# Loading q and k in whole 4 KB runs, in transfers of 512 KB, in a sliding-window attention and mixture-of-adapters kernel

## The chip, the core and the metric

The kernel runs on one core of one Trainium2 chip. The metric is the device time of one execution in microseconds (us). A core has five engines that work side by side: TensorE (PE in the profile, with its weight loads as PEld), VectorE (DVE), ScalarE (ACT), GpSimd (POOL) and SyncE (SP). Sixteen DMA engines move data between the chip's memory and the core.

## The reference

Sliding-window attention over 8 batches, 8 heads, 576 rows and 64 columns, followed by a mixture of eight rank-16 adapters of which each row takes the best two:

```python
scores = scale * np.matmul(q, k.transpose(0, 1, 3, 2))
mask = np.abs(pos[:, None] - pos[None, :]) <= 32
scores = np.where(mask, scores, -1000000000.0)
attn = softmax(scores)                       # rows
x = (attn @ v) with heads beside each other  # 4608 x 512
logits = x @ w_gate                          # 8 experts
topk, w = best two experts of a row, softmax of their logits
out = x + sum over the two of w * ((x @ A[e]) @ B[e])
```

The inputs q, k and v are float32, 9.4 MB each; the output is 9.4 MB.

## The kernel before, in words

**Tiling.** The 8 batches are taken as 4 stages `s`; each stage holds the batches `s` and `s + 4` (the two groups `g`) side by side. Along the rows a batch is cut into 256-row pieces `t` (two for each stage, `t` = 0 to 7) and a remainder piece `t` = 8 (`XT`) that gathers the last rows (for q the first and the last rows) of all heads and batches. For each piece there is a q tile and a k tile; both come as *halves* `hf` = 0 and 1.

**Loading q and k** (`load_qk`, `run_parts`). A partition belongs to a run of 16 rows of one head, 4 KB of memory in one piece. A half takes 8 of these 16 rows, so each partition's packet has 2 KB, and a half is two transfers (one for each group) of 256 KB, four of 128 KB for q of the remainder. They are issued on SP's queue (L317) into one of nine buffers `raw`. Each half is then cast to float16 into `c16` (L328 on ACT, L330 on DVE or POOL), turned by eight transposing matmuls (L338), and copied from PSUM into `qT` or `kT` (L355). `ends` (L365) copies the remainder's q rows to where the stage's first and last blocks need them.

**Loading v** (`load_v`). Four transfers for each piece, issued on POOL's queue (L383), read 8 KB of float32 for each of 32 partitions and write 4 KB of float16 into `v16`; a VectorE transpose (L391) makes `vt` of it. There are 36 such transfers.

**Computing.** `score` puts mask (L426) and scores (L432) into two PSUM banks, and ACT takes the exponential into `PT` (L438). `pv` multiplies `PT` with `vt` (L478), and DVE normalises into `xa` or `xb` (L490, L497). `moe` transposes these rows (L523, L182), computes gate and first adapter product (L563), the gate on DVE and ACT (L573 to L604), transposes again (L613), computes the second product and adds x (L637, L640), and evicts into one of four buffers `ob` (L648, L651); SP stores them (L658), two transfers for each `ob`.

**Order.** Nothing is scheduled at run time. Every step is an `Op`; `Plan.give` issues them in the order of the table `ORDER`, with the engine from `ON` and the buffer from `HOME`. These three tables were found by a search. Every engine works through its own steps in that order and waits where a step isn't ready, so what stands behind a waiting instruction on the same engine waits too. Transfers on SP's queue rotate over eight completion semaphores, shared with the three weight loads on ACT's queue: a transfer is issued only after the eighth transfer before it has landed.

Of the kernel before, what the change touches and what calls it, by code (L numbers as in the profile page):

```python
# [16 lines left out]
D = 64  # L17
# [86 lines left out]
def kernel(  # L104
# [14 lines left out]
    POOLS = {"B": 8, "raw": 9, "c16": 6, "v16": 3, "xq": 1,  # L119
# [5 lines left out]
    def many(name, shape, dt, pool=sb):  # L125
# [3 lines left out]
        "raw": many("raw", [128, 2, 8 * D], F32),  # L129
# [158 lines left out]
    def run_parts(w, t, f):  # L288

        r = []  # L290
        for g in range(2):
            x = grows[w][g]
            if t < XT:
                r0 = 256 * (t % 2) + (32 if w == "q" else 0)
                i = x[t // 2, :, r0:r0 + 256].rearrange("h (n f r) d -> f n h (r d)", f=2, r=8)[f]
                r.append((g, 0, 128, i))
            elif w == "k":
                i = x.rearrange("b h n d -> (b h) n d")[:, 512:576].rearrange(
                    "u (n f r) d -> f u n (r d)", f=2, r=8)[f]
                r.append((g, 0, 128, i))  # L300
            else:
                for e in range(2):
                    i = x.rearrange("b h n d -> (b h) n d")[:, 544 * e:544 * e + 32].rearrange(
                        "u (n f r) d -> f u n (r d)", f=2, r=8)[f]
                    r.append((g, 64 * e, 64, i))
        return r

    def load_qk(w, t):
# [4 lines left out]
        dst = kT[t] if w == "k" else xq if t == XT else qT[t // 2]  # L313
        for hf in range(2):
            raw = buf("raw", f"raw{w}{t}_{hf}")
            for n, (g, p0, np_, src) in enumerate(run_parts(w, t, hf)):
                op("SP", 0.46, lambda g=g, p0=p0, np_=np_, src=src, raw=raw: nc.sync.dma_start(  # L317
                    out=ap(raw)[p0:p0 + np_, g], in_=src),
                   bufs=[raw], make=[(w, t, "raw", hf)],
                   prio=(-80 + due + late if t else -200 + late) + 0.1 * hf + 0.01 * n,  # L320
                   dma=DMA_MB / 4 * np_ / 128, desc=np_)
            c16 = buf("c16", f"{w}16_{t}_{hf}")

            def cast(eng, raw=raw, c16=c16):
                o = ap(c16).rearrange("p r (g d) -> p r g d", g=2)
                i = ap(raw).rearrange("p g (r d) -> p r g d", d=D)
                if eng == "ACT":
                    nc.scalar.copy(out=o, in_=i)  # L328
                else:
                    (nc.vector if eng == "DVE" else nc.gpsimd).tensor_copy(out=o, in_=i)  # L330
            op({"DVE": 0.68, "ACT": 1.03} if t == 0 else CAST, 0,
               cast, bufs=[raw, c16],
               need=[(w, t, "raw", hf)], make=[(w, t, hf, "16")], prio=due - 30 + late + 0.1 * hf)
# [345 lines left out]
def BY_PE(s, w, j):  # L679
# [36 lines left out]
)  # L716
ON = (
    "001110000000100000000100010001000000010000000010000001000100000000000000000101000100000100"
    "001000010000000110010000000000000000100000000000000000001000100010000000000000000010000000"
    "000000000100000000000001000000000000000000000000010001000000000000000101000000000000000000"  # L720
    "001000001000000000000010000000000000000000000100000000000000000000010000100000100000010010"
    "000100100000001000000000011000001000000000000010000100000000000100000100000100010010000000"
    "000000000000000000010000000000000000000000100000000000000000000000000000000000000100000000"
    "0000000000000000000000000000000000000000100000000001000"
)
HOME = (
# [13 lines left out]
)  # L740


# [1 line left out]
_INS = ['q', 'k', 'v', 'moe_w_gate', 'moe_A', 'moe_B']  # L744
_OUTS = [((4608, 512), 'float32')]


# [23 lines left out]
```

## Time and profile before

| | |
|---|---|
| median of 3 runs | 150.35 us (149.16 to 151.33) |
| the profiled execution: its time, its span | 149.54 us, 147.8 us |
| PE busy | 117.6 us (80%) |
| DVE, ACT, POOL busy | 90.4, 84.9, 51.6 us |
| moved by DMA | 33.91 MB in 19,783 packets |
| read from memory, written to it | 28.85 MB, 9.44 MB |

The profile is of one execution. Busy time is the time in which an engine runs an instruction; the span is that of the instructions on the core, and the execution's own time is 1.7 us longer. A DMA packet is what one DMA engine moves in one go; the DMA share is the packets' time over the time of all 16 engines, and as packets overlap a little it can pass 1. The chain of work is followed back from the last instruction: at each step to what released it.

### The profile page before, as it was taken

How to read it: one execution, taken by the hardware profiler on the slowest of the kernel's cores; microseconds unless marked ns; L12 is line 12 of the kernel's file. 1: busy time of each engine (PE TensorE's matmuls, PEld its weight loads, DVE VectorE, ACT ScalarE, POOL GpSimd, SP SyncE). 2: the span in 40 equal slices, each digit the busy share in tenths (PEclk: the TensorE clock that was granted, in tenths of full speed). 3: DMA queues.
4: the chain of work that ended last, by engine and by line, in shares of the span. 5: the costliest groups of instructions: out<-in, count | busy, mean ns of one | idle time of the engine just before them, and what ended most of it. 6: DMA issues, size and time to landing. Idle time of an engine off the chain costs nothing.

```text
span 147.8 us, 5212 instructions
## 1 busy us (share of the span) xinstructions
PE 117.6 (80%) x2206; PEld 85.0 (58%) x2206; DVE 90.4 (61%) x185; ACT 84.9 (57%) x123; POOL 51.6 (35%) x88
## 2 busy tenths in 40 slices
PE   4932279869399789599899999999998999976730
PEld 2302265656198657486488794677685674954300
DVE  4010067080568567997997764786958589958530
ACT  4102434937644896568666839659697588542530
POOL 7960002853388225623529139940200000000000
PEclk9995556999968999959999999999999999999995
DMA  4999999999999999999999999999911030940484
GB/s 128 256 225 254 266 254 297 283 258 254 271 273 273 275 240 277 268 286 347 326 278 322 302 301 290 145 266 293 332 40 49 27 113 0 320 150 0 170 311 160
DMA packets 19783, 33.91 MB, mean 230 GB/s; under 512 B 4656, under 2 KB 4656, under 8 KB 19760
## 3 DMA queue, kind: packets, MB, share of 16 engines
q1 hardware_dynamic: 15680, 28.32, 63.5%
q0 software_dynamic: 2752, 4.72, 18.0%
q10 hardware_dynamic: 1328, 0.54, 1.6%
q8 instruction: 17, 0.28, 0.8%
q14 instruction: 6, 0.05, 0.1%
HBM read 28.85 MB, written 9.44 MB: 259 GB/s over the span
## 4 chain that ended last, share of the span: by engine, by line
PE 54%; DMA 20%; DVE 13%; ACT 3%; issue 3%; POOL 2%; SPq 0%; DVEq 0%; ACTq 0%; POOLq 0%
PE banks L432 11%; DMA raw<-in_q_dram 9%; PE banks L338 8%; PE banks L478 8%; PE banks L426 6%; DMA v<-in_v_dram 6%; PE banks L523 6%; PE banks L637 5%; PE banks L563 5%; DMA raw<-in_k_dram 4%; DVE xb L497 4%; PE banks L640 3%; DVE vt L391 3%; PE banks L613 2%; DVE ob L648 1%
## 5 line engine op out<-in xcount | busy, mean ns | idle before, releaser
L330 POOL CAST c<-raw 128x1024 f16<-128x1024 f32 x26 | 26.7, 1045 | 50.5 <-DMA raw<-in_k_dram 27.4
L438 ACT ACTIVATE PT<-banks 128x1024 f16<-128x1024 f32 x36 | 35.7, 1026 | 7.9 <-PE banks L432 7.4
L338 PEld LDWEIGHTS <-c 128*128 128x128 f16 x288 | 20.2, 111 | 12.6 <-ACT c L328 8.5
L338 PE MATMUL banks<-swap,c 128*128 128x128 f16 x256 | 21.2, 242 | 6.9 <-ACT c L328 4.7
L391 DVE STREAM_TRANSPOSE vt<-v 128x1024 f32<-128x1024 f32 x9 | 18.4, 2061 | 7.2 <-DMA v<-in_v_dram 7.2
L432 PE MATMUL banks<-qT,kT 64*64 64x128 f16 (+1 forms) x576 | 22.2, 218 | 0.6 <-ACT qT L355 0.4
L432 PEld LDWEIGHTS <-kT 64*64 64x64 f16 x576 | 16.8, 108 | 10.2 <-issue 9.3
L478 PE MATMUL banks<-vt,PT 64*128 64x65 f16 x832 | 17.8, 192 | 6.0 <-DVE vt L391 3.0
L478 PEld LDWEIGHTS <-PT 64*128 64x128 f16 x832 | 14.9, 95 | 9.4 <-issue 7.3
L383 POOL DMA_DIRECT2D v<-in_v_dram x36 | 19.6, 559 | 0.7 <-DVE sm L574 0.6
L497 DVE TENSOR_TENSOR xb<-banks,rc 128x768 f16<-128x768 f32 x16 | 15.3, 958 | 3.4 <-PE banks L523 3.0
L637 PE MATMUL banks<-Bw,zT 128*128 128x512 f16 x40 | 14.4, 381 | 1.7 <-ACT zT L182 1.7
L426 PE MATMUL banks<-mask,twice 64*128 64x512 f16 x72 | 14.9, 390 | 0.5 <-ACT qT L355 0.4
L328 ACT CAST c<-raw 128x1024 f16<-128x1024 f32 x7 | 7.3, 1044 | 12.2 <-DMA raw<-in_k_dram 6.7
L355 ACT COPY qT<-banks 128x512 f32<-128x512 f32 x14 | 8.1, 588 | 10.5 <-PE banks L338 8.1
L648 ACT COPY ob<-banks 128x1024 f32<-128x1024 f32 x11 | 11.1, 1020 | 4.0 <-PE banks L640 3.4
L182 ACT COPY xT<-banks 128x512 f32<-128x512 f32 x15 | 8.6, 588 | 5.9 <-PE banks L523 5.2
L330 DVE CAST c<-raw 128x1024 f16<-128x1024 f32 x3 | 2.1, 694 | 15.9 <-DMA raw<-in_q_dram 14.9
L355 ACT COPY kT<-banks 128x512 f32<-128x512 f32 x13 | 7.7, 589 | 6.5 <-PE banks L338 6.5
L563 PE MATMUL banks<-WA,xT 128*128 128x136 f16 x160 | 10.8, 223 | 0.0
L497 DVE TENSOR_TENSOR xa<-banks,rc 128x640 f16<-128x640 f32 (+1 forms) x12 | 10.3, 862 | 0.3
L563 PEld LDWEIGHTS <-xT 128*128 128x128 f16 x160 | 9.6, 98 | 0.6
(61 smaller groups left out, 130.5 us busy)
## 6 DMA issues: line engine op xcount, KB each, us to landing
raw<-in_k_dram SPq DMA_DIRECT2D x36, 256.0 KB, 7.1
raw<-in_q_dram SPq DMA_DIRECT2D x32, 256.0 KB, 7.4
out_dram<-ob SPq DMA_DIRECT2D x24, 256.0 KB, 4.3
v<-in_v_dram POOLq DMA_DIRECT2D x36, 128.0 KB, 7.2
out_dram<-ob SPq DMA_DIRECT2D x16, 192.0 KB, 3.2
raw<-in_q_dram SPq DMA_DIRECT2D x8, 128.0 KB, 7.1
ob<-in_moe_A_dram ACTq DMA_DIRECT2D x1, 256.0 KB, 3.7
ob<-in_moe_B_dram ACTq DMA_DIRECT2D x1, 256.0 KB, 5.4
```

The lines of the kernel that those rows point to most:

```text
L330: (nc.vector if eng == "DVE" else nc.gpsimd).tensor_copy(out=o, in_=i)
L338: nc.tensor.matmul(out=ap16(tp)[:, 128 * r:128 * r + 128], lhsT=ap(c16)[:, r], rhs=swap if t < XT else ident, is_transpose=True, start=Tru ...
L355: (nc.vector.tensor_copy if eng == "DVE" else nc.scalar.copy)(out=o, in_=i)
L383: op("POOL", 0.5, lambda p0=p0, src=src: nc.gpsimd.dma_start(out=ap(v16)[p0:p0 + 32], in_=src), bufs=[v16], make=[("v", t, "16")], prio=-6 ...
L391: nc.vector.transpose(out=o, in_=i)
L426: nc.tensor.matmul(out=p[:, 4 * j:4 * j + 4], lhsT=twice[m], rhs=bcast(mask[m], 1, 4), start=True, stop=False)
L432: nc.tensor.matmul(out=p[m, h, c0:c0 + hi - lo], lhsT=ap(kT[t])[m, 64 * sl:64 * sl + 64], rhs=ap(qT[s])[m, h, lo:hi], start=False, stop=h ...
L438: op("ACT", act(1024), lambda: nc.scalar.activation(out=ap(pt)[:, :, 64:192].rearrange("m i (x b r) -> m i x b r", b=2, r=16), in_=ap(ps). ...
L478: nc.tensor.matmul(out=ap(po)[:, 512 * g + VD * j:512 * g + VD * j + VD], lhsT=ap(PT[ti])[m, pos, off:off + 128], rhs=ap(vt[t])[m, sl, 0:V ...
L497: nc.vector.tensor_tensor(out=o, in0=i, in1=ap(rc)[:, 0:n].to_broadcast([128, n, 2, D]), op=ALU.mult)
L563: nc.tensor.matmul(out=ap(pz)[:, o:o + ER + E], lhsT=ap(xT)[:, i, c, :], rhs=WA[:, c, :], start=(c == 0), stop=(c == 3))
L637: nc.tensor.matmul(out=o, lhsT=ap(zT)[:, j + i], rhs=Bw, start=True, stop=not by_pe)
```

## The change

A q or k piece is loaded whole. `run_parts` no longer takes the half `f`: each partition's packet is the whole run of 16 rows, 4 KB, and a transfer has 512 KB (256 KB for q of the remainder). A `raw` buffer is twice as large (8 KB for each partition) and there are five of them, where there were nine. The two casts of a piece read the two halves of one `raw` buffer, and both need all transfers of the piece. Casts, transposes, evictions and everything behind them keep their shapes and their number. 76 load transfers of q and k become 40. The three tables `ORDER`, `ON` and `HOME` come from a new search, so the order of all steps, the engine of some, and the buffers are others. Line numbers behind `run_parts` are three lower.

```diff
-    POOLS = {"B": 8, "raw": 9, "c16": 6, "v16": 3, "xq": 1,
+    POOLS = {"B": 8, "raw": 5, "c16": 6, "v16": 3, "xq": 1,
...
-        "raw": many("raw", [128, 2, 8 * D], F32),
+        "raw": many("raw", [128, 2, 16 * D], F32),
...
-    def run_parts(w, t, f):
+    def run_parts(w, t):
...
-                i = x[t // 2, :, r0:r0 + 256].rearrange("h (n f r) d -> f n h (r d)", f=2, r=8)[f]
+                i = x[t // 2, :, r0:r0 + 256].rearrange("h (n r) d -> n h (r d)", r=16)
                 r.append((g, 0, 128, i))
...
+        raw = buf("raw", f"raw{w}{t}")
+        for n, (g, p0, np_, src) in enumerate(run_parts(w, t)):
+            op("SP", 0.46, lambda g=g, p0=p0, np_=np_, src=src: nc.sync.dma_start(
+                out=ap(raw)[p0:p0 + np_, g], in_=src),
+               bufs=[raw], make=[(w, t, "raw")],
+               prio=(-80 + due + late if t else -200 + late) + 0.01 * n,
+               dma=DMA_MB / 2 * np_ / 128, desc=np_)
         for hf in range(2):
-            raw = buf("raw", f"raw{w}{t}_{hf}")
-            for n, (g, p0, np_, src) in enumerate(run_parts(w, t, hf)):
-                op("SP", 0.46, lambda g=g, p0=p0, np_=np_, src=src, raw=raw: nc.sync.dma_start(
-                    out=ap(raw)[p0:p0 + np_, g], in_=src),
-                   bufs=[raw], make=[(w, t, "raw", hf)],
...
-            def cast(eng, raw=raw, c16=c16):
+            def cast(eng, hf=hf, c16=c16):
                 o = ap(c16).rearrange("p r (g d) -> p r g d", g=2)
-                i = ap(raw).rearrange("p g (r d) -> p r g d", d=D)
+                i = ap(raw).rearrange("p g (f r d) -> p f r g d", f=2, d=D)[:, hf]
...
-               need=[(w, t, "raw", hf)], make=[(w, t, hf, "16")], prio=due - 30 + late + 0.1 * hf)
+               need=[(w, t, "raw")], make=[(w, t, hf, "16")], prio=due - 30 + late + 0.1 * hf)
...
 ORDER = (
...
 ON = (
...
 HOME = (
```

More of the change, by code (lines that the diff above doesn't have):

```diff
@@ L294, in run_parts @@
                 r0 = 256 * (t % 2) + (32 if w == "q" else 0)
-                i = x[t // 2, :, r0:r0 + 256].rearrange("h (n f r) d -> f n h (r d)", f=2, r=8)[f]
+                i = x[t // 2, :, r0:r0 + 256].rearrange("h (n r) d -> n h (r d)", r=16)
                 r.append((g, 0, 128, i))
[L297 to L305, printed above, removed]
+                continue
+            u = x.rearrange("b h n d -> (b h) n d")
+            rows = [(0, 512, 576)] if w == "k" else [(0, 0, 32), (64, 544, 576)]
+            for p0, a, b in rows:
+                i = u[:, a:b].rearrange("u (n r) d -> u n (r d)", r=16)
+                r.append((g, p0, 2 * (b - a), i))
         return r
@@ L313, in load_qk @@
         dst = kT[t] if w == "k" else xq if t == XT else qT[t // 2]
-        for hf in range(2):
-            raw = buf("raw", f"raw{w}{t}_{hf}")
-            for n, (g, p0, np_, src) in enumerate(run_parts(w, t, hf)):
-                op("SP", 0.46, lambda g=g, p0=p0, np_=np_, src=src, raw=raw: nc.sync.dma_start(
-                    out=ap(raw)[p0:p0 + np_, g], in_=src),
-                   bufs=[raw], make=[(w, t, "raw", hf)],
-                   prio=(-80 + due + late if t else -200 + late) + 0.1 * hf + 0.01 * n,
-                   dma=DMA_MB / 4 * np_ / 128, desc=np_)
+        raw = buf("raw", f"raw{w}{t}")
[5 more added lines that the diff above has]
+               dma=DMA_MB / 2 * np_ / 128, desc=np_)
+        for hf in range(2):
             c16 = buf("c16", f"{w}16_{t}_{hf}")
-            def cast(eng, raw=raw, c16=c16):
+            def cast(eng, hf=hf, c16=c16):
                 o = ap(c16).rearrange("p r (g d) -> p r g d", g=2)
-                i = ap(raw).rearrange("p g (r d) -> p r g d", d=D)
+                i = ap(raw).rearrange("p g (f r d) -> p f r g d", f=2, d=D)[:, hf]
                 if eng == "ACT":
@@ L684 @@
 ORDER = (
[31 rows of a table removed]
[29 rows of a table added]
 )
 ON = (
[L718 to L724, printed above, removed]
+    "000001101001100000000000010000000010000101000100100011000100000000000000000011101100001010"
+    "000000100000000100000010100000000000000000010010000000000001001001000000100000000000000000"
+    "000000000010000000000000000000000000100100100000000000000000000000000100000000000000000010"
+    "100000000100000000000001000000000000011000000000100000001000000000000000001010000000000000"
+    "010000000100000000000000000011100001000000100000000010000100000000000000000000100000000010"
+    "010000000000000000000000000010000000000000010000000000000000000000000000000000000000000001"
+    "00000000000001000"
 )
 HOME = (
[13 rows of a table removed]
[12 rows of a table added]
 )
```

85 rows, old and new, of tables (HOME, ORDER) are left out of this document.

## The prediction

> **What bounds the kernel now.** I read the page first, for engines and DMA queues.
>
> ```profile
> span 147.8 us, 5212 instructions
> PE 117.6 (80%) x2206; PEld 85.0 (58%) x2206; DVE 90.4 (61%) x185; ACT 84.9 (57%) x123; POOL 51.6 (35%) x88
> ...
> DMA  4999999999999999999999999999911030940484
> ...
> q1 hardware_dynamic: 15680, 28.32, 63.5%
> q0 software_dynamic: 2752, 4.72, 18.0%
> ...
> q8 instruction: 17, 0.28, 0.8%
> ```
>
> The DMA engines are full from the second of 40 slices to the 29th, about 107 us; only then have the last loads landed. PE is busy 80% of the whole. So I ask where PE is short of work, with the windows cut at the end of the warm-up matmuls, the first score, the start of PE's dense part, and the last evictions (columns: length, busy time of PE, PEld, DVE, ACT, POOL, granted clock, DMA share, GB/s):
>
> ```profile
> 8.60:23.70 15.10, 6.00 (x51) 4.72 (x50) 4.49 (x9) 4.51 (x6) 1.45 (x3) 0.58 1.07 259
> 23.70:64.00 40.30, 32.42 (x693) 25.73 (x693) 24.98 (x43) 25.77 (x38) 21.99 (x32) 0.92 1.07 266
> 64.00:128.00 64.00, 62.12 (x1333) 45.29 (x1332) 49.34 (x101) 46.19 (x65) 20.71 (x27) 0.99 0.76 224
> 128.00:147.80 19.80, 10.67 (x140) 6.74 (x132) 9.74 (x27) 6.02 (x11) 0.00 (x0) 0.91 0.49 166
> ```
>
> Three regimes. Up to 23.7 us the loads bound: DMA share 1.07, PE idle 9.1 us. From 23.7 to 64 loads and PE share the bound: PE idles 7.9 us while the DMA share stays at 1.07. From 64 to 128 PE is the bound, with 1.9 us idle in 64. The last 19.8 us are a chain of small steps with no load in it. The chain of waits, in order of time, shows the first two:
>
> ```profile
> 1.47 6.26 DMA raw<-in_k_dram
> 7.75 6.95 DMA raw<-in_q_dram
> 14.72 6.84 DMA raw<-in_q_dram
> 21.62 1.05 ACT c L328
> 22.72 1.03 PE banks L338 x8
> 23.76 0.54 PE banks L426
> ...
> 29.67 8.80 DMA v<-in_v_dram
> 38.50 2.05 DVE vt L391
> 40.59 0.70 PE banks L478 x34
> ```
>
> Faster loads can therefore win time only ahead of about 64 us: what PE idles there is the most that they can give.
>
> **What a packet costs.** From the DMA view of a window with q and k loads alone (20 to 26 us), of one with v beside them (8 to 21.6), and of one with stores (124 to 147):
>
> ```profile
> q1 hardware_dynamic: 954, 1.74, 106.4%
> ...
> q0 software_dynamic: 480, 0.79, 29.9%
> ...
> q1 hardware_dynamic: 2256, 4.06, 51.2%
> ```
>
> Load of 2 KB: 1.74 MB are 849 data packets (the rest of the 954 tell of completion); 16 engines x 6 us x 1.064 / 849 = 120 ns of engine time, 113 ns elapsed. Read of 8 KB (v): 0.79 MB are 192 packets that write 4 KB and read 8 KB; 0.299 x 16 x 13.6 us / 192 = 339 ns. Store of 2 KB: 4.06 MB are 1,982 packets; 0.512 x 16 x 23 us / 1,982 = 95 ns.
>
> The change makes 4 KB reads, which this trace doesn't show. From below: half of v's 8 KB, 170 ns. From above, without gain, two of 120, 240 ns. A loss isn't excluded: the 17 instruction packets (q8) of 16 KB took 0.008 x 16 x 147.8 us / 17 = 1,113 ns, or 278 ns for 4 KB. I take the straight line between the two load rows, 120 + (339 - 120)/3 = 193 ns: it uses the same direction and engines, while the instruction packets are few and go by another queue.
>
> [...]
>
> **The change part by part.**
>
> *Load time in total.* 18.87 MB of q and k are 576 packets of 2 KB for each engine, 576 x 113 = 65.1 us of the 107 us. As 288 packets of 193/1.064 = 181 ns they take 52.2 us: 12.9 us less (19.1 less at 170 ns, 0 at 240, 10.1 more at 278). The last q and k pieces would land some 13 us earlier if the queue stays fed; but PE, saturated from 64 us, can't use most of it.
>
> *The first score.* It needs q and k of piece 0, and in both orders q of the remainder is turned ahead of it on PE: 3.15 MB, 96 packets of 2 KB for each engine, 10.8 us, now 48 x 181 = 8.7 us: -2.1 us (-3.1 to +1.7). In the new order POOL issues seven v transfers ahead of the mask, not six: one more, 2 x 339/1.064 ns for each engine, +0.6. The two casts of the remainder's q now come free together and both stand on ACT, one behind the other; before, only the second was left when its half landed (21.62 in the chain). That is one cast more, 1.05 us. Together -0.5 us (-1.4 to +3.4), all of it on the path.
>
> *From the first score to 64 us.* PE's waits in this stretch:
>
> ```profile
> PE banks L478 <- DVE vt L391: 2.6, 1, 2.6
> PE banks L478 <- DVE ob L651: 1.7, 1, 1.7
> PE banks L523 <- DVE xb L497: 1.4, 2, 0.8
> PE banks L478 <- issue: 1.3, 1, 1.3
> ```
>
> The first is v's second piece, the v transfer of the chain. The second is indirectly a load: DVE waits for v, then transposes twice, and the eviction stands behind. v's transfers are late because POOL issues them behind casts that wait for q and k, and because they share the engines with them:
>
> ```profile
> POOL c L330 <- DMA raw<-in_k_dram: 27.4, 7, 13.7
> ```
>
> The new order keeps that form: the fourth transfer of v's second piece stands on POOL behind the four casts of q1 and k1. They wait now for whole pieces, 2.1 MB more behind the remainder's q: 32 packets x 181 ns = 5.8 us, and some 3 us of v between, so k1 is there at about 21.1 + 9 = 30, cast by 32, against the issue at 29.67 before. This wait isn't shortened. What is won is that all q and k behind it come a fifth faster. I take 3.5 us of the 7.9 us; the ends are 0 and 7.9.
>
> *Edits at nothing.* SP issues 36 loads less, each some 0.54 us (minimum, median and longest in ns, by the view of the raw tiles):
>
> ```profile
> L317 SPq DMA_DIRECT2D raw<-in_q_dram x40: 528/537/1415, 0.7 to 97.0; - x40
> ```
>
> SP isn't on the path but for the first issue; the full DMA rings hide the others, and without that cover each costs its 0.54. Two casts go from ACT to POOL, same length, covered by POOL's 35%. PE's work is unchanged; its clock of 0.92 in the middle may rise a little (0 to 2.6 us, taken as 0). The stretch from 64 to 128 keeps its 62 us, and the end, where the new order has the same steps behind the last scores, its 19.8 us.
>
> *Sum.* 147.8 - 0.5 - 3.5 = 143.8 us of span; with the 1.74 us around it in the profiled execution (149.54 against 147.8) 145.5 us. That execution stands 0.8 us under the median of the runs, 150.35; I leave this in the range. About 2% can be told from no change here: faster means under 147.3, slower over 153.4.
>
> **The rivals.**
>
> *All idle time goes.* The loads run so far ahead that PE is dense from the first score: 147.8 - 1.4 - 7.9 + 1.7 = 140.2 us. For it: DMA share 1.07 through all of that stretch. Against: of the four waits above, 1.4 and 1.3 us belong to DVE and PSUM banks, not to loads.
>
> *No gain in a packet.* The engine's bytes set the time, 240 ns. Then the first score is 1.7 us later (0.6 + 1.05), nothing else moves: 149.54 + 1.7 = 151.2 us. For it: the largest packets of the trace, the 16 KB of q8, took longer per byte than those of 2 KB, so size alone doesn't make a packet fast. Against: 120 ns against 95 ns for the same 2 KB.
>
> *Slower: stores queue behind twice the bytes.* SP's queue holds eight transfers. Now these are at most 2.1 MB, which at 290 GB/s is 7.2 us, and the landing times say the same:
>
> ```profile
> raw<-in_k_dram SPq DMA_DIRECT2D x36, 256.0 KB, 7.1
> raw<-in_q_dram SPq DMA_DIRECT2D x32, 256.0 KB, 7.4
> ...
> out_dram<-ob SPq DMA_DIRECT2D x12, 256.0 KB, 6.4
> ...
> out_dram<-ob SPq DMA_DIRECT2D x7, 192.0 KB, 5.3
> ```
>
> (The last two rows are of 60 to 105 us.) With eight of 512 KB ahead, 4.2 MB at 362 GB/s, a store lands after 11.6 us instead of 6.4. In those 45 us 19 stores empty 9.5 of the four `ob`, one each 4.7 us, so a buffer may be held 18.9 us: eviction 1.2, two issues 1.1, landing 11.6, which leaves 5.0 us for SP's wait ahead of the store. On SP, loads that wait for one of only five `raw` buffers stand between the stores. From the point at which such a wait passes 5 us, the eviction waits for `ob`, holds its two PSUM banks, and PE stops in the stretch that has no slack. At 1 us for each of 9.5 fills: 145.5 + 9.5 = 155.0 us. Against: loads and stores alternate in the new order there, so fewer than eight large ones are ahead.
>
> **How the numbers follow.** The forecast, 145.5 us, has 0.55, with its own range 142 to 149 (a fifth of it above 147.3); all idle time gone 0.10; no gain 0.17; stores late 0.18. Faster: 0.8 x 0.55 + 0.10 = 0.54. Within 2%: 0.11 + 0.14 of the no-gain case + 0.02 of the late stores = 0.27. Slower: 0.03 + 0.16 = 0.19. The range reaches from just under the first rival, 139.5, to past the second and halfway to the third, 153.5; outside lie about a tenth above and less than that below.
>
> **What the changed profile would show.** Right: q and k packets of 4 KB at some 193 ns (share and count of q1); DMA full up to some 95 us and not 107; first score (L423, formerly L426) near 23 us; PE idle of 4 to 5 us from there to 64. No gain: packets of 240 ns, DMA full to 107 again. Late stores: landing of stores past 11 us, and waits of an `ob` eviction for a store. The forecast is wrong if PE idles in the dense part, 64 to 128, for more than some 2 us, or if the tail grows beyond 20 us: both would come from the new order, which this profile can't show.

## The result and the profile after

The changed kernel takes 166.09 us, median of its runs (165.24 to 166.43), against 150.57 us of the kernel before on the same chip: a ratio of 1.103 (1.094 to 1.113; such a pair behind a ratio is a 95% interval). It is slower by a tenth where 145.5 us were forecast, and the range ended at 153.5. Some executions of a kernel run in a slower state of the core; every ratio in this document leaves them out, so below it need not be the quotient of two medians. The profiled execution took 166.1 us with a span of 164.3.

The page of the changed kernel, its busy times, the slices and the queues:

```profile
span 164.3 us, 5141 instructions
...
PE 118.9 (72%) x2206; PEld 85.8 (52%) x2206; DVE 92.6 (56%) x187; ACT 81.8 (50%) x119; POOL 53.6 (33%) x90
...
DMA  4999993999999999999999999991040046271285
...
q1 hardware_dynamic: 10464, 28.32, 61.3%
```

PE works 1.3 us longer than before; the other 15.2 of the 16.5 us are idle time of PE. Two things stand out in the DMA line: it is full to the 27th slice of 4.1 us, some 111 us (forecast 95), and the seventh slice, at 25 to 29 us, has a hole. The third is in the queues: q1 has 5,216 packets less and yet holds the engines for 0.613 x 16 x 164.3 = 1,611 us, where it held them for 0.635 x 16 x 147.8 = 1,502. With the stores at the prediction's 95 ns each (438 us for 4,608), an estimate, the loads took 1,064 / 9,216 = 115 ns a packet before and take 1,174 / 4,608 = 255 ns now. Twice the packet costs 2.2 times the time. A window of the changed kernel that holds no stores, 34 to 50 us, says the same:

```profile
q1 hardware_dynamic: 1099, 3.99, 98.0%
```

3.99 MB are 974 packets of 4 KB; 0.98 x 16 x 16 us / 974 = 258 ns, where the kernel before showed 120 ns for 2 KB.

The windows, cut as in the prediction:

```profile
8.60:23.70 15.10, 3.78 (x32) 3.25 (x32) 4.83 (x9) 1.04 (x1) 3.54 (x9) 0.54 1.09 214
23.70:64.00 40.30, 25.79 (x445) 19.60 (x446) 14.89 (x27) 17.41 (x27) 16.49 (x23) 0.70 0.97 229
64.00:128.00 64.00, 56.43 (x1244) 42.30 (x1242) 49.59 (x93) 43.87 (x64) 25.85 (x34) 1.00 0.81 223
128.00:164.30 36.30, 26.51 (x482) 18.14 (x482) 21.55 (x50) 17.80 (x26) 0.00 (x0) 0.94 0.45 154
```

PE idles 11.3 us in the first row (before 9.1), 14.5 in the second (7.9), 7.6 in the third (1.9) and 9.8 in the last (9.1): 2.2 + 6.6 + 5.7 + 0.7 = 15.2 us. The engines moved 229 GB/s in the second row, where they moved 266 before.

The chain of waits from its start names what comes first:

```profile
1.64 24.82 DMA ob<-in_moe_A_dram
27.08 6.42 DMA raw<-in_q_dram
33.51 20.66 DMA raw<-in_q_dram
...
55.31 9.10 DMA v<-in_v_dram
64.53 1.14 DVE vt L388
```

The waits of SP's queue (us in total, times, longest) tell why a small weight load stands there:

```profile
SPq L313 <- DMA ob<-in_moe_A_dram: 19.4, 1, 19.4
```

And the issues of the page, with the landing time in the last column:

```profile
raw<-in_k_dram SPq DMA_DIRECT2D x18, 512.0 KB, 13.5
raw<-in_q_dram SPq DMA_DIRECT2D x16, 512.0 KB, 11.4
...
v<-in_v_dram POOLq DMA_DIRECT2D x36, 128.0 KB, 10.6
...
ob<-in_moe_A_dram ACTq DMA_DIRECT2D x1, 256.0 KB, 24.8
```

The new order issues the gate weights first on ACT's queue, then B, then A (before: A first, landed after 3.7 us). A is 1,024 packets of 256 B. Behind the others it took 24.8 us. In the trace the 81 transfers that SP and ACT issue share eight completion semaphores, and none goes out before the earlier one on its semaphore has landed. The first load of the second q piece had A's: it went out at 26.48 us, 0.02 us after A's landing, and SP had stood for 19.4 us. When A landed, at 26.5 us, the engines had run dry: that is the hole. Landing times of q and k went from 7.1 and 7.4 us to 13.5 and 11.4, and v's, whose transfers did not change, from 7.2 to 10.6.

### The profile page after: what moved, and what is told of

Its sections match the earlier page's. It is cut to its first block, busy times and chain, and to the rows that moved or that the text cites. A ratio compares the mean times of both kernels' runs of the same rounds, so it can differ in the third digit from the quotient of the medians.

```text
span 164.3 us, 5141 instructions
## 1 busy us (share of the span) xinstructions
PE 118.9 (72%) x2206; PEld 85.8 (52%) x2206; DVE 92.6 (56%) x187; ACT 81.8 (50%) x119; POOL 53.6 (33%) x90
## 4 chain that ended last, share of the span: by engine, by line
PE 42%; DMA 37%; DVE 10%; issue 4%; ACT 2%; ACTq 1%; SPq 0%; POOL 0%; DVEq 0%; POOLq 0%
DMA raw<-in_q_dram 16%; DMA ob<-in_moe_A_dram 15%; PE banks L429 8%; PE banks L475 6%; DMA v<-in_v_dram 6%; PE banks L335 5%; PE banks L634 5%; PE banks L560 5%; PE banks L423 5%; PE banks L520 4%; PE banks L637 3%; DVE xb L494 3%; DVE xa L494 2%; PE banks L610 1%; ACT PT L435 1%
## 5 line engine op out<-in xcount | busy, mean ns | idle before, releaser
L327 POOL CAST c<-raw 128x1024 f16<-128x1024 f32 x28 | 28.5, 1049 | 51.6 <-DMA raw<-in_q_dram 36.3
L335 PEld LDWEIGHTS <-c 128*128 128x128 f16 x288 | 19.8, 110 | 23.9 <-ACT c L325 11.9
L429 PE MATMUL banks<-qT,kT 64*64 64x128 f16 (+1 forms) x576 | 23.7, 225 | 0.3 <-ACT qT L362 0.2
L429 PEld LDWEIGHTS <-kT 64*64 64x64 f16 x576 | 17.8, 112 | 10.9 <-issue 10.7
L475 PE MATMUL banks<-vt,PT 64*128 64x65 f16 x832 | 18.3, 197 | 1.9 <-issue 1.5
L475 PEld LDWEIGHTS <-PT 64*128 64x128 f16 x832 | 15.8, 99 | 4.8 <-issue 3.2
L182 ACT COPY xT<-banks 128x512 f32<-128x512 f32 x16 | 9.1, 589 | 15.3 <-PE banks L520 13.0
L325 ACT CAST c<-raw 128x1024 f16<-128x1024 f32 x5 | 5.2, 1049 | 19.3 <-DMA raw<-in_q_dram 10.1
L487 DVE RECIPROCAL rc<-banks 128x12 f32<-128x12 f32 (+1 forms) x28 | 6.2, 223 | 11.0 <-PE banks L475 10.5
L327 DVE CAST c<-raw 128x1024 f16<-128x1024 f32 x3 | 2.0, 691 | 13.4 <-DMA raw<-in_k_dram 10.6
## 6 DMA issues: line engine op xcount, KB each, us to landing
raw<-in_k_dram SPq DMA_DIRECT2D x18, 512.0 KB, 13.5
raw<-in_q_dram SPq DMA_DIRECT2D x16, 512.0 KB, 11.4
v<-in_v_dram POOLq DMA_DIRECT2D x36, 128.0 KB, 10.6
ob<-in_moe_A_dram ACTq DMA_DIRECT2D x1, 256.0 KB, 24.8
```

Of the source, the lines that this page charges most:

```text
L335: nc.tensor.matmul(out=ap16(tp)[:, 128 * r:128 * r + 128], lhsT=ap(c16)[:, r], rhs=swap if t < XT else ident, is_transpose=True, start=Tru ...
L429: nc.tensor.matmul(out=p[m, h, c0:c0 + hi - lo], lhsT=ap(kT[t])[m, 64 * sl:64 * sl + 64], rhs=ap(qT[s])[m, h, lo:hi], start=False, stop=h ...
L475: nc.tensor.matmul(out=ap(po)[:, 512 * g + VD * j:512 * g + VD * j + VD], lhsT=ap(PT[ti])[m, pos, off:off + 128], rhs=ap(vt[t])[m, sl, 0:V ...
```

## The experiments

Three suspects: A's place, the depth of a transfer (512 KB), and the packet. All ratios are to the kernel before, run on the same chip in the same job.

### Weights first; and the reverse in the kernel before

`e1_a_first`, the changed kernel with A, B and the gate weights issued first:

```diff
 ORDER = (
-    4, 26, 27, 5, 1, 18, 11, 0, 10, 25, 31, ...
+    25, 27, 26, 4, 5, 1, 18, 11, 0, 10, 31, ...
```

> The changed kernel, but the three weight loads on ACT's queue are issued in the order of before: A first, then B, then the gate. Theory 'blocked queue': in the changed kernel A's load comes third, its 256 B packets take turns with 4 KB packets of q, k and v and land only at 26.5 us, and SP's next load waits 19.4 us for that load's completion semaphore. With A first it lands near 4 us, as before; SP issues q1 by 9 us and not at 26.5, and the time falls by 8 to 14 us, to 152 to 158 us. Rival 'large packets': the loads are slow because a 4 KB packet takes 254 ns, more than two of 2 KB, and nothing waits for A that the full DMA engines don't delay anyway; the time stays above 163 us.

`e2_before_a_last`, the kernel before with the gate weights first, then B, then A (`25, 4, 7, ...` becomes `26, 27, 25, 4, 7, ...`):

> The kernel before, but the three weight loads in the order of the changed kernel: gate, B, A. Blocked queue: A's 64 packets for each engine take turns with 2 KB packets of some 120 ns and v's of 322 ns, so A lands at some 15 to 20 us; the loads on SP behind its semaphore stall for 5 to 10 us, the DMA engines run dry in between, and the time rises by 3 to 8 us, to 153 to 159 us. Large packets: nothing to do with it, the time stays at 150 to 151 us.

Measured: 160.95 us, ratio 1.079 (1.054 to 1.105), and 151.24 us, ratio 1.019 (1.004 to 1.034). Both moved in the expected direction and by less. In the second, SP waited only 1.3 us for A, where 5 to 10 were expected. The landing times of the first:

```profile
raw<-in_k_dram SPq DMA_DIRECT2D x18, 512.0 KB, 15.5
raw<-in_q_dram SPq DMA_DIRECT2D x16, 512.0 KB, 14.2
...
v<-in_v_dram POOLq DMA_DIRECT2D x36, 128.0 KB, 9.7
...
ob<-in_moe_A_dram ACTq DMA_DIRECT2D x1, 256.0 KB, 3.5
```

A lands after 3.5 us and the hole is gone, but q and k still need 14 to 16 us: A's place is some 2.4 of the 10.3 points. In the kernel before, whose q and k packets have 2 KB, A landed after 6.9 us though it was last.

### Depth and packet apart

`e3_cut_by_halves` is the kernel with weights first, each load issued as two of 256 KB whose packets are the 2 KB halves of a run; the two casts still wait for all of a piece:

```diff
-            op("SP", 0.46, lambda g=g, p0=p0, np_=np_, src=src: nc.sync.dma_start(
-                out=ap(raw)[p0:p0 + np_, g], in_=src),
+            def both(g=g, p0=p0, np_=np_, src=src):
+                for f in range(2):
+                    cols = slice(8 * D * f, 8 * D * f + 8 * D)
+                    nc.sync.dma_start(out=ap(raw)[p0:p0 + np_, g, cols], in_=src[:, :, cols])
+            op("SP", 0.46, both,
```

> The kernel of the first run (A first), but each load of a whole piece is issued as two transfers of 256 KB that take the first and the second 8 rows of each run: packets of 2 KB again, everything else (order, buffers, casts waiting for the whole piece) as there. Beside its twin, cut by partitions, it differs in the packet alone. If 4 KB packets are no faster than two of 2 KB, the two are within 1.5 us of each other; if they are faster (193 against 240 ns, the forecast), this one is slower than the twin by 4 us or more; if they are slower (254 against 240), it is faster by 1 to 4 us.

`e4_cut_by_partitions` issues two transfers of 64 partitions each, with 4 KB packets:

```diff
+                    nc.sync.dma_start(out=ap(raw)[p0:p0 + m, g], in_=src[:c])
+                    nc.sync.dma_start(out=ap(raw)[p0 + m:p0 + np_, g], in_=src[c:])
```

> The kernel of the first run (A first), but each load is issued as two transfers of 64 partitions: packets of 4 KB, transfers of 256 KB. Against the first run it differs in the transfer size alone: eight transfers in flight are 2 MB and not 4 MB. If the deep queue costs (stores and the next needed piece land later), it is faster than the first run by 2 us or more; if the transfer size is of no account, the two are within 1.5 us.

`e5_cut_by_heads` issues two transfers of four heads each (16 groups of 4 runs, 4 KB packets), the permutation matrix following:

```diff
+                    part = src[:, c * f:c * f + c] if t < XT else src[c * f:c * f + c]
+                    nc.sync.dma_start(out=ap(raw)[p0 + m * f:p0 + m * f + m, g], in_=part)
```

> The kernel of the first run (A first), each load issued as two transfers of 256 KB that take four heads each: packets of 4 KB, and 16 engines for each transfer, which the cut by partitions did not keep (its runs of 8 by 8 went to 8 engines). Beside the cut by halves (152.9 us) it differs in the packet alone, beside the first run (161.0 us) in the transfer alone. Theory 'packet': 4 KB packets take turns with v's and push v and the stores back, whatever the transfer's size; it stays at 158 to 163 us. Rival 'depth': what costs is eight transfers of 512 KB in flight; it comes down to 152 to 155 us.

Measured: e3 152.91 us, ratio 1.032 (1.019 to 1.045); e4 182.34 us, 1.206 (1.177 to 1.235); e5 155.22 us, 1.049 (1.033 to 1.065). Landing times, of e3 and then of e5:

```profile
raw<-in_k_dram SPq DMA_DIRECT2D x36, 256.0 KB, 8.0
raw<-in_q_dram SPq DMA_DIRECT2D x32, 256.0 KB, 9.1
```

```profile
raw<-in_k_dram SPq DMA_DIRECT2D x36, 256.0 KB, 7.5
raw<-in_q_dram SPq DMA_DIRECT2D x32, 256.0 KB, 9.2
```

With half the transfer the landing time falls to about half for k (from 15.5 us in e1) and to two thirds for q (from 14.2), with either packet. From e1 to e5 the depth is halved: 3.0 points. Each transfer of e5 also writes only one half of the partitions, but among the loads alone below that was no dearer (288 against 287 ns). From e5 to e3, 4 KB to 2 KB, are 1.7 points. The intervals overlap, so neither size is firm; a gain of the larger packet is in neither step. e4 does not answer its question, because its transfers seem to have run on eight engines, by a count. Of q1's 10,560 packets there 9,216 carry data, and 1,344 are small ones (of 4 B in the traces before and after). The kernel before has 15,680 - 13,824 = 1,856 of these for 116 transfers, 16 for each. At 16, e4's 40 stores and 12 remainder transfers have 640 and 192; that leaves 512 for the other 64, eight for each. The same cut among the loads alone, below, held the 16 engines at 51%.

### Two checks of the weights

`e6_halves_a_last` is e3 with the changed kernel's own order (A last); `e8_before_weights_on_pool` is the kernel before with the weights issued on POOL's queue behind the first six v transfers (`nc.scalar.dma_start` becomes `nc.gpsimd.dma_start` for the three).

> The cut by halves (2 KB packets, 152.9 us) with the weight loads in the order of the changed kernel, A last. Blocked queue with the packet's size in it: A's 64 packets for each engine take turns with packets half as long, so A lands near 14 to 18 us and not at 26.5, and the time rises by 1 to 3 us. If the delay of A hangs on v's early transfers alone, A lands past 22 us and the time rises by 4 us or more, as between the changed kernel and the first run (5 us).

> The kernel before, with the three weight loads issued on POOL's queue behind the first six v transfers: they no longer stand ahead of the first q and k packets, and no longer use three of the eight completion semaphores that SP's loads share. If both cost at the start, the first score comes 1 to 2 us earlier and the time is 148 to 149 us where before has 150; if not, or if POOL's issue of 1,024 small packets delays its casts, it is the same or up to 2 us slower.

Measured: 155.0 us, ratio 1.054 (1.039 to 1.069), so that A's place costs some 2.2 points with 2 KB packets too (the intervals overlap); and 150.73 us, 1.019 (1.010 to 1.028): the other queue is no cure. SP's wait in e6:

```profile
SPq L316 <- DMA ob<-in_moe_A_dram: 4.6, 1, 4.6
```

A's landing there, from the issues:

```profile
ob<-in_moe_A_dram ACTq DMA_DIRECT2D x1, 256.0 KB, 10.0
```

SP waits 4.6 us, not 19.4, and in the kernel before (e2) 1.3, and the cost is the same 2 points within the intervals. So the long wait did not cost its length. What the place of the weight loads does cost in these runs is not shown; with the deep loads much was late with or without the wait (e1).

### Casts that wait for half a piece

`e9_cast_by_halves` is e3 with the transfers in the order of the halves, and a buffer of its own for each half:

```diff
-        "raw": many("raw", [128, 2, 16 * D], F32),
+        "raw": list(zip(many("rawa", [128, 2, 8 * D], F32, n=5), many("rawb", [128, 2, 8 * D], F32, n=5))),
...
+                for g, p0, np_, src in parts[n % m::m]:
+                    nc.sync.dma_start(out=ap(raw)[f][p0:p0 + np_, g], in_=src[:, :, cols])
...
-                i = ap(raw).rearrange("p g (f r d) -> p f r g d", f=2, d=D)[:, hf]
+                i = ap(raw)[hf].rearrange("p g (r d) -> p r g d", d=D)
```

> The kernel with weights first and 2 KB packets in 256 KB transfers (1.032 of the kernel before), with two more edits: a piece's transfers go out by halves (both groups of the first half, then of the second), and each cast reads a buffer of its own that only its half's transfers fill. The order of all steps stays that of the changed kernel. If the remaining 3% are casts that wait for whole pieces: the ratio falls to 1.00 to 1.015, and the windows show PE idle under 8 us between 23.7 and 64 us. If they are the new order: the ratio stays at 1.025 to 1.04, PE idle there some 9 us as in that kernel (40.3 - 31.5).

Measured: 152.33 us, ratio 1.018 (1.010 to 1.026), between the two theories; its interval overlaps that of e3. The windows of 23.7 to 64 and 64 to 128 us:

```profile
23.70:64.00 40.30, 32.57 (x678) 24.18 (x677) 26.19 (x43) 26.55 (x40) 21.11 (x29) 0.87 1.07 273
64.00:128.00 64.00, 59.28 (x1239) 43.84 (x1236) 48.18 (x99) 43.22 (x62) 21.42 (x27) 1.00 0.70 212
```

PE idles 7.7 us in the first, as in the kernel before (7.9), and 4.7 in the second (1.9 before). What is left of the loss, 1.8 points, lies by exclusion in the new tables; no run shows it directly.

### Loads alone: what a packet costs

Why does a 4 KB packet cost more than two of 2 KB? Four runs, `m1` to `m4`, issue loads of q and k on SP's queue, 8.4 MB a stage or more, with none of the kernel's computing. Each run was executed once.

```python
def whole_runs():                    # the changed kernel's way: 16 groups of 8 runs
    x = (q, k)[n % 2][n // 2 % 8, :, 0:256].rearrange("h (n r) d -> n h (r d)", r=16)
def half_runs():                     # the same with 2 KB; double_runs: with 8 KB
def whole_runs_in_line():            # 128 runs that follow each other in memory
nc.sync.dma_start(out=raw[n % N][:, 0:1024], in_=x)
```

> Loads of q and k alone, on SP's queue, 8.4 MB in each of seven stages, with a reader between them; no attention and no experts are computed, and the output is zero. The stages: 2 KB packets (half runs), 4 KB packets (whole runs, 512 KB), 4 KB cut by partitions, 4 KB cut by heads, 8 KB packets, 4 KB in the order of memory, 2 KB again. Forecast of the prediction: 2 KB 120 ns, 4 KB 193 ns, 8 KB 339 ns of engine time a packet. Rival 'bytes': 4 KB and 8 KB take two and four times as long as 2 KB, 240 and 480 ns, since what 16 engines together get from memory is the bound; then all stages on 16 engines run at 260 to 290 GB/s.

The DMA view of five windows: 4 KB the kernel's way (40 to 58 us), 4 KB cut by heads (118 to 145), 8 KB (160 to 195), 4 KB in line (231 to 247), 2 KB the kernel's way (253 to 277):

```profile
q1 hardware_dynamic: 1162, 4.22, 102.8%
...
q1 hardware_dynamic: 1892, 6.20, 100.9%
...
q1 hardware_dynamic: 1074, 7.80, 101.5%
...
q1 hardware_dynamic: 1789, 6.52, 102.3%
...
q1 hardware_dynamic: 3466, 6.31, 105.0%
```

By the working of the prediction (bytes give the data packets, share x 16 x length the engines' time) these are 287 ns for 4 KB the kernel's way, 288 cut by heads, 597 for 8 KB, 165 for 4 KB in line, and 131 for 2 KB: 223 to 263 GB/s for the kernel's way, 407 GB/s in line. In the kernel's way a KB costs 66 ns with 2 KB packets, 72 with 4 KB and 75 with 8 KB; in line it costs 41. So the rival 'bytes' is nearer to the prices than the forecast, but the rate that it names as the bound of 16 engines together is none: in line they get half as much again and more. The stage cut by partitions held the engines at a share of 51% (84 to 100 us), half of the time of 16, which fits the eight engines of e4's count. The next run varied where the runs lie:

```python
def neighbours_in_a_block(): x = rows(n)[...128 runs...].rearrange("(i o) e -> o i e", o=16)
def heads_outside():         x = (q, k)[n % 2][b:b + 2, :, r0:r0 + 128].rearrange("b h (n r) d -> (b h) n (r d)", r=16)
def apart_with_jumps():      # groups 32 KB apart, 1,152 KB from one run of a group to the next
```

> Loads alone, nothing of the reference is computed. Sixteen transfers of 512 KB with 4 KB packets in each stage, which differ in the address distance between the 16 engines and between the packets of one engine: in line (32 KB, 4 KB), the kernel's way (4 KB, 144 KB), neighbours within one block (4 KB, 64 KB), heads outside (144 KB, 4 KB), apart with jumps (32 KB, 1,152 KB), in line again. If 16 engines reading neighbouring runs at once are what costs: the second and third stage take some 245 ns a packet, the others some 170. If it is the jump from one packet of an engine to its next: second, third and fifth some 245, first, fourth and last some 170. If it is neither: only the in-line stages are at 170, since their transfers are one piece of memory.

The kernel's way (26 to 56 us), heads outside (97 to 125), in line (160 to 174):

```profile
q1 hardware_dynamic: 2040, 7.44, 102.8%
...
q1 hardware_dynamic: 1977, 7.21, 103.1%
...
q1 hardware_dynamic: 1575, 5.74, 102.8%
```

272, 262 and 164 ns; the two other places are like the first two. Only the in-line transfers are fast, so neither distance is the cause. The third run took the form instead: runs at one pitch in memory without being in line, and groups of 8 that nearly are.

```python
def every_eighteenth(): x = rows(n).rearrange("(p s) e -> s p e", s=18)[n // 2]            # one pitch, 72 KB
def nearly_in_line():   x = rows(n)[...144 runs...].rearrange("(o s) e -> o s e", s=9)[:, 0:8]
def in_line_strips():   # 2 KB halves of runs at one pitch
```

> Loads alone, nothing of the reference is computed. Stages of 8.4 MB from q and k: 512 KB in line; 128 runs of 4 KB at a pitch of 8 KB; the same at 72 KB; 16 groups of eight runs that follow each other, with one run left out between groups; 2 KB halves of 4 KB runs (256 KB transfers); in line again. The stages before showed 166 ns a packet in line and some 250 for every transfer that is described as 16 groups of 8 runs, wherever these lie. If it is the place in memory that costs: the fourth stage, which is nearly in line, is at 170, those at 8 and 72 KB pitch at some 245. If it is the description in two levels, the fourth is at 245 and the second and third at 170. If every transfer that isn't one piece of memory is slow: 245 in all but the first and last, 120 for the 2 KB halves.

At 72 KB pitch (46 to 60 us), nearly in line (66 to 90), 2 KB at one pitch (98 to 112):

```profile
q1 hardware_dynamic: 1576, 5.74, 102.7%
...
q1 hardware_dynamic: 1878, 6.85, 102.2%
...
q1 hardware_dynamic: 2976, 5.42, 105.5%
```

164, 235 and 89 ns. The place in memory matters little: 128 runs at one pitch are fast in line, at 8 KB (165 ns) and at 72 KB, and 16 groups of 8 are slow even when all but in line, if somewhat less so (235 ns, 286 GB/s). The last run asked whether it is the description or the partitions that an engine writes:

```python
def in_line_64(halves): # 64 runs in line into partitions 0-63; or 0-63 and 64-127 by turns
def shift():            # loads of 12 x 4, 8 x 4 and 4 x 4 packets ahead of the kernel's way
def groups(a, b):       # a groups of b runs: 32 x 4, 64 x 2
```

> Loads alone, nothing of the reference is computed. 4 KB packets throughout: 512 KB in line; 64 rows in line into partitions 0 to 63 only (256 KB); the same into 0 to 63 and 64 to 127 by turns; the kernel's way (16 groups of 8 runs); three small loads on 12, 8 and 4 engines, then the kernel's way again; 32 groups of 4 runs; 64 groups of 2 runs; in line again. If two engines that write neighbouring partitions get in each other's way, and that is why the kernel's way stands at 270 ns and 250 GB/s and in line at 164 ns and 410: the 64 rows in line into one half of the partitions fall to some 215 GB/s although nothing else about them changes, and the small loads, which set one engine of each such pair four packets behind the other, bring the kernel's way to 165 ns. If it is the description in two levels: the 64 rows stay at 400 GB/s, the small loads change nothing, 32 by 4 and 64 by 2 stand at 250 GB/s too. [...]

Partitions 0 to 63 only (30 to 60 us), the kernel's way with the small loads ahead (140 to 162), 32 groups of 4 (172 to 188), 64 groups of 2 (192 to 208):

```profile
q1 hardware_dynamic: 1914, 6.27, 103.5%
...
q1 hardware_dynamic: 1538, 5.61, 103.1%
...
q1 hardware_dynamic: 1803, 6.55, 102.7%
...
q1 hardware_dynamic: 1798, 6.56, 102.8%
```

324, 265, 164 and 164 ns; the 64 rows into both halves by turns (68 to 98 us) took 302. Neither theory holds whole. The partitions count: the same in-line packets into half of them take twice as long (209 GB/s against 410). But the small loads changed nothing (265 ns with and without them, the latter at 106 to 130 us), and a description in two levels is no brake by itself: 32 groups of 4 are as fast as in line (164 ns, 410 GB/s). The trace holds neither a packet's engine nor its partition, so whether the small loads shifted the engines against each other is not shown, and why 16 groups of 8 are slow stays open.

### The cure, in both kernels

`e10_before_32_groups` is the kernel before with a half cut by heads: 32 runs of 8 rows for each of four heads. The packets stay 2 KB and the transfers 256 KB:

```diff
-                i = x[t // 2, :, r0:r0 + 256].rearrange("h (n f r) d -> f n h (r d)", f=2, r=8)[f]
+                i = x[t // 2, 4 * f:4 * f + 4, r0:r0 + 256].rearrange("h (n r) d -> n h (r d)", r=8)
...
-        blk = swap.rearrange("p (h n) -> p h n", n=16)
+            blk = swap.rearrange("p (h x f b) -> p f h x b", h=4, f=2, b=2)[:, f]
...
-                    i = ap(tp).rearrange("m (r h x) -> m h x r", r=8, h=NH)
+                    i = ap(tp).rearrange("m (r h x) -> m h x r", r=8, h=4)
```

> The kernel before with the same packets (2 KB) and transfers (256 KB), but a half is now four heads with all their 8-row runs, described as 32 groups of 4, where it was eight heads with every second 8-row run, 16 groups of 8; the permutation matrix and the eviction follow, the order of the steps stays. If the form of the transfer, by which partitions an engine writes, held the loads back in the kernel: q and k packets fall from 120 ns to some 90, the loads end some 10 to 15 us earlier than at 104 us, and the ratio is 0.93 to 0.98, since PE has 7.9 us of idle time between 23.7 and 64 us and 9.1 ahead of it. If it only holds where nothing else moves (v's transfers, which keep their form, and the stores beside them): 0.98 to 1.01 and packets of 110 ns or more.

`e11_new_order_32_groups` gives e9 the same loads.

> The kernel with weights first, 2 KB packets, casts by halves and the order of the changed kernel (1.018 of the kernel before), with the same 32 groups of 4. If the last 2% are the new order waiting for loads: the ratio falls by as much as in the kernel before with this form, or more, and the two come within 1% of each other. If the new order costs by itself: this one stays 1.5 to 2.5% above that one.

Measured: 144.48 us, ratio 0.975 (0.965 to 0.985), faster than both kernels; and 147.35 us, 0.987 (0.971 to 1.004), which can't be told from the kernel before. Of e10, the DMA view of 20 to 26 us, q and k loads alone:

```profile
q1 hardware_dynamic: 1276, 2.32, 105.4%
```

And the windows of e10:

```profile
8.60:23.70 15.10, 7.72 (x68) 5.73 (x68) 5.53 (x8) 5.21 (x8) 2.95 (x5) 0.55 1.06 292
23.70:64.00 40.30, 34.52 (x710) 27.15 (x708) 25.34 (x50) 27.30 (x42) 22.40 (x33) 0.87 0.94 271
64.00:128.00 64.00, 61.65 (x1363) 45.46 (x1363) 50.16 (x99) 44.21 (x62) 19.57 (x26) 1.00 0.74 222
```

2.32 MB are 1,133 packets of 89 ns, against 120 in the same window of the kernel before. PE idles 7.4 us (9.1) and 5.8 (7.9) in the first two rows, and 2.3 (1.9) in the third. So the form did hold the loads back in the kernel itself, with 2 KB packets. One part of the expectation missed: the loads end only some 3 us earlier (the last cast of a q or k piece starts at 101.7 us, before at 104.5); SP issues the last of them at 93.7 us, before at 97.0. e11 won 3.1 points from the form and stays 1.3 above e10, between its two theories; the intervals overlap, so an own price of the new order of that size is likely and not shown. No run gave the changed kernel 4 KB packets in 32 groups of 4, so whether whole runs pay in that form is open.

## Why the prediction was wrong, step by step

**What bounds the kernel** was read rightly: faster loads do win time ahead of 64 us (e10), and slower ones lost 8.8 of the 15.2 us of idle time there.

**What a packet costs** is the first step that failed: 193 ns forecast, 255 measured, past the 240 of "no gain" and inside the outer bound of 278. The straight line took size for the cause and joined two rows of different forms: v's 8 KB reads go by POOL's queue into 32 partitions, with a cast. Within the form of q and k, the loads alone took 131 ns for 2 KB, 272 to 287 for 4 KB and 597 for 8 KB: no slope to win on. What could have warned stood in the prediction: 2 KB stores took 95 ns and 2 KB loads 120, so something other than the size held the loads.

**Load time in total**: in place of 12.9 us less, the engines' time of the loads rose from 1,064 to 1,174 us, some 7 us more on each of 16 engines. In a good form, too, size had little to give: at one pitch (m3) 2 KB at 89 ns are nearly as fast for a byte as 4 KB at 164 (387 against 410 GB/s).

**The first score**, near 23 us by forecast. PE's timeline of the changed kernel:

```profile
27.27 0.61 PE L423 MATMUL banks<-mask,twice 64*128 64x512 f16 x2
```

27.3 us, +3.6 and just past the end that was given (+3.4). In e1, e3 and e9 it stood at 27.8, 27.8 and 27.4 us, so neither A nor packet nor depth set it. The order did: with the same loads in groups of 4, the old order (e10) has it at 21.9 us and the new one (e11) at 26.8.

```profile
L430 PE MATMUL banks<-mask,twice x72: 372/386/606, 21.9 to 118.2; 64*128 64x512 f16 x72
...
L431 PE MATMUL banks<-mask,twice x72: 372/387/612, 26.8 to 122.7; 64*128 64x512 f16 x72
```

The step took the new way to the first score as the old one with two terms added, and miscounted one of them: it counted the v transfers ahead of the mask, seven for six. POOL's timelines, of the kernel before (first row) and of the changed one:

```profile
6.19 3.64 POOL L383 DMA_DIRECT2D v<-in_v_dram  x6
...
1.82 1.79 POOL L380 DMA_DIRECT2D v<-in_v_dram  x3
...
6.10 2.19 POOL L380 DMA_DIRECT2D v<-in_v_dram  x4
...
10.25 0.55 POOL L380 DMA_DIRECT2D v<-in_v_dram  x1
...
15.73 0.53 POOL L380 DMA_DIRECT2D v<-in_v_dram  x1 [1.59 <-DMA v<-in_v_dram]
```

With two single ones between the last two rows, eleven v transfers go out ahead of the first score, not seven: five more than before. At the prediction's own price, 0.64 us each, they are 3.2 us where it put 0.6; no run changed this count alone.

**From the first score to 64 us**: 3.5 us to be won, 6.6 lost. The wait that was followed, POOL's casts of q1 and k1 ahead of v's second piece, was the right one. Its row in the changed kernel:

```profile
POOL c L327 <- DMA raw<-in_q_dram: 36.3, 4, 17.4
```

q1's loads waited for A's semaphore and landed at 33.5 us (the chain). k1, expected at 30 and cast by 32, was cast from 39.3 to 41.4 us, and the v transfer behind it went out at 41.3, not near 32; a later one, behind a q piece that took 20.7 us to land, at 55.3. The rotation over eight semaphores, shared by SP and ACT, was known; what the step left out is that the new order moves A's issue to the third place on ACT's queue.

**Edits at nothing**: no run tells the price of the 36 issues or of the moved casts. "The stretch from 64 to 128 keeps its 62 us" failed (56.4): PE idles 7.6 us there, past the 2 us that the prediction named as a sign of being wrong. It laid that to the new order; but in the new order the idle time falls to 3.8 us with 2 KB packets (e3) and 2.9 with the better form (e11), so most of it is likely that of late loads. The tail held: its last 19.8 us, from 144.5, hold 10.0 us of PE, before 10.7.

**The rivals.** "No gain in a packet" was nearest for the packet, which cost a little more than two of 2 KB (1.7 points, 2.6 us, from e5 to e3). That its price reads 1.7 us is chance: it added up one v transfer and one cast, and put the packet itself at nothing. The third rival had the depth, some 3.0 points, but sought its harm at the stores: their landings grew (7.7 and 9.7 us in 60 to 105 us, from 6.4 and 5.3) without passing 11 in the median, and no row there has PE waiting for them; the loads themselves and v came late. A's place (2.4 points) was no rival at all. In points of the time before: 10.3 = 2.4 (A) + 3.0 (depth) + 1.7 (packet) + 1.4 (casts on whole pieces, e3 to e9) + 1.8 (order). The intervals of neighbouring steps overlap, so the single terms are rough. Even if depth and packet together (4.7 points) were all the packet's, the other parts would be 5.6, so more than half of the loss is likely not the packet's.

## What to carry to other kernels

A packet's price belongs to the form of its transfer (here 164 to 324 ns for the same 4 KB): before drawing a line through two rows, see whether both write as many partitions, in the same groups, by the same queue. Here transfers twice as large landed later (q's after 11.4 us, not 7.4), and so did v's on another queue (10.6, not 7.2); so follow each DMA that a new order moves to the semaphore that the next issue needs, and count the transfers that it puts ahead of the first result. Where a load to 128 partitions runs at 250 GB/s in 16 groups, try to describe it by 32 or 64 groups or at one pitch (387 to 410 GB/s here) before changing its size.

## What the runs showed of the hardware

- Loads alone (m1 to m4): 128 partitions loaded as 16 groups of 8 runs moved 223 to 263 GB/s with 2, 4 or 8 KB packets (286 when the groups were all but in line); as 32 groups of 4, 64 of 2, or at one pitch 387 to 410 GB/s, and at one pitch whether the runs lay in line or 72 KB apart.
- 256 KB of 256 B packets, last of three on its queue, landed after 24.8 us (the changed kernel) where q's and k's packets had 4 KB, after 10.0 (e6) and 6.9 us (e2) where they had 2 KB, and after 3.5 us when it was first (e1).
- In-line loads into partitions 0 to 63 alone took 324 ns for a 4 KB packet, twice the 164 ns of 128 partitions (m4).
